# First MLP layer as seven products of half blocks, and the two MLP layers as two stages with their activations in DRAM

## The chip, the cores and the metric

The kernel runs on one core of a Trainium2 chip. Its engines are TensorE (PE in the profile, with its weight loads listed as PEld), VectorE (DVE), ScalarE (ACT), GpSimd (POOL) and SyncE (SP), which issues all DMAs of this kernel. The metric is the time of one execution on the device in microseconds (us), the median of several; lower is better.

## What is computed

An attention over 8 batches, 8 heads, 576 positions of width 64, masked by blocks of 64 positions, is followed by a layer norm and an MLP of two layers (512 to 2048 to 512) with a residual. All inputs and outputs are float32.

```python
scores = scale * np.matmul(q, k.transpose(0, 1, 3, 2))
scores = np.where(block_i >= block_j, scores, -1000000000.0)
attn = np.exp(scores - np.max(scores, axis=-1, keepdims=True))
attn = attn / (np.sum(attn, axis=-1, keepdims=True) + 1e-09)
x = np.matmul(attn, v)            # heads side by side: (8, 576, 512)
xn = (x - mu) / np.sqrt(var + 1e-06) * g_ln
ch = np.maximum(xn @ w_ch1, 0.0) @ w_ch2
return (x + ch).astype(np.float32)
```

The weights arrive as 64-bit words, because the arrays are double precision on the host, and the kernel turns them into float32 on the chip.

## The kernel before

**Order.** Nothing is issued where it is written. Every operation is handed to a planner (`Plan.add`) with its engine or a choice of engines, a cost in us, what it reads and writes, and a priority; `Plan.run` plays the program through with those costs and writes each engine's instructions in the order in which it took them. On the chip each engine then works through its own list strictly in that order and stands still at an instruction whose inputs are not there. A choice of engines (`any_of`, as for the copies out of PSUM in `evac`) is settled by the planner too.

**Attention.** `pair` is called for 32 pairs of heads. On PE a pair is scores (L390), transposes of the softened scores (L417) and the products with the values (L423, L427), with scores one pair ahead of the rest (`pe` and `plan.chain` fix PE's order). DVE takes maxima out of PSUM (L405), ACT the exponentials (L408), both share the copies (L218, L220), and DVE turns the output block (L499, a transpose into `ot`), which SP stores to `xd` in DRAM (L501). `first` does the 64 leading positions of eight pairs at a time. `decode` turns weights into float32 during attention: ACT, POOL, DVE steps on a 128x512 tile (L321 to L333), then a high part (a copy to fp32r, L218 or L220) and a low part (the difference, on POOL, L346), kept in SBUF as `w1h`, `w1l`, `w2h`, `w2l`.

**MLP.** `mlp(n)` handles 4 tiles of 128 tokens, 9 times. Each tile is loaded from `xd`, scaled by the attention's sums (L617), its mean and variance taken (L623, L624), reduced by the mean and multiplied by `g` (L628), turned (L633), stored to and loaded from DRAM in the turned layout, and split into `xh` and `xl`. Then, for each of 16 column blocks j of the hidden layer, PE does 12 matmuls of the first layer (three per 128 rows of input: high by high, high by low, low by high, L680 to L682), ACT and DVE split the rectified result into `hh` and `hl` (L688, L690), and PE does 12 matmuls of the second layer on them (L697 to L699), which add up in PSUM over j. DVE multiplies by the inverse deviation and adds the residual (L706), SP stores (L709). The hidden activations never leave the core.

A matmul of the first layer, and one of the second, move 512 columns:

```python
nc.tensor.matmul(hp.t, w1h[:, c, jf], xh.t[:, c], start=(c == 0), stop=False)
nc.tensor.matmul(ys[s].t, hh.t[:, sl], w2h, start=(j == 0), stop=False)
```

There are 9 x 16 x 12 = 1728 of each layer.

## Time and profile before

| | |
|---|---|
| median of 3 runs | 1100.79 us (1100.09 to 1101.01) |
| profiled execution, first to last instruction (its span) | 1099.8 us |
| PE busy | 1087.7 us, 99% of the span |
| PE weight loads busy | 874.2 us, 79% |
| DVE busy | 517.9 us, 47% |
| ACT busy | 357.5 us, 33% |
| POOL busy | 129.5 us, 12% |

The span is that of one execution, from its first to its last instruction; the times in the first line are of other executions and hold about 1 us more. Busy times are sums of recorded durations. A matmul's recorded duration runs on into that of the next one (they are pipelined), so what a matmul costs in a dense stretch is read from the distance between two starts, not from its duration. The clock column of a window is TensorE's granted clock as a share of 2.4 GHz; 0.50 is its other level, 1.2 GHz.

### The profile page before, as it was taken

What the parts mean: (1) busy time and instruction counts of PE and PEld (TensorE: products, weight loads), DVE (VectorE), ACT (ScalarE), POOL (GpSimd) and SP (SyncE); (2) the same over time, 40 slices, a digit from 0 to 9 for tenths busy, and PEclk for the clock granted to TensorE, in tenths of its full rate; (3) what the DMA queues carried; (4) which work ended last, traced back from release to release, by engine and by line L of the source; (5) the groups of instructions that cost most, each with busy time, mean ns of one, the idle gap of its engine ahead of it and who ended that gap; (6) DMA issues with size and microseconds to landing.
All of it is one profiled execution on the core that took longest, in us unless ns stands there. A gap on an engine that the chain in (4) does not pass through costs nothing.

```text
span 1099.8 us, 16300 instructions
## 1 busy us (share of the span) xinstructions
PE 1087.7 (99%) x6288; PEld 874.2 (79%) x6288; DVE 517.9 (47%) x1192; ACT 357.5 (33%) x884; POOL 129.5 (12%) x192
## 2 busy tenths in 40 slices
PE   9999999999999999999999999999999999999998
PEld 6777777777778888888888888888888888888886
DVE  6899888786775235136126116216315414512111
ACT  8878898898633111111111111111111111111110
POOL 1243432231025101001001001000000100100000
PEclk9999999999999999999999999999999999999999
DMA  6787755655353033024015005104204203301000
GB/s 209 222 217 223 238 190 185 226 168 169 102 129 97 20 78 76 1 63 91 1 43 100 12 1 124 29 1 106 48 1 96 58 1 84 70 1 39 1 1 38
DMA packets 205085, 97.80 MB, mean 89 GB/s; under 512 B 155728, under 2 KB 184400, under 8 KB 205008
## 3 DMA queue, kind: packets, MB, share of 16 engines
q1 hardware_dynamic: 205008, 96.76, 32.3%
q8 instruction: 49, 0.80, 0.3%
q14 instruction: 28, 0.23, 0.1%
...
## 4 chain that ended last, share of the span: by engine, by line
PE 88%; ACT 4%; DVE 4%; DMA 1%; issue 1%; POOL 1%; SPq 0%; DVEq 0%; ACTq 0%; POOLq 0%
PE hp L680 12%; PE hp L682 12%; PE hp L681 12%; PE y L699 12%; PE y L698 11%; PE y L697 11%; PE s L390 5%; PE tr L417 5%; PE o L427 5%; PE o L423 2%; ACT pt L218 1%; ACT pab L408 1%; ACT pu L408 1%; DVE pab L405 1%; DMA st_w2l<-w 1%
## 5 line engine op out<-in xcount | busy, mean ns | idle before, releaser
L690 DVE SCALAR_TENSOR_TENSOR hhl<-hp,hhl 128x512 fp32r<-128x512 f32 x144 | 99.5, 691 | 451.1 <-ACT hhl L688 450.8
L688 ACT ACTIVATE hhl<-hp 128x512 fp32r<-128x512 f32 x144 | 86.1, 598 | 678.3 <-PE hp L682 678.3
L699 PE MATMUL y<-w2h,hhl 128*128 128x512 f32 x576 | 224.4, 390 | 0.3 <-DVE hhl L690 0.3
L698 PE MATMUL y<-w2l,hhl 128*128 128x512 f32 x576 | 224.4, 390 | 0.0
L697 PE MATMUL y<-w2h,hhl 128*128 128x512 f32 x576 | 224.3, 389 | 0.0
L699 PEld LDWEIGHTS y<-w2h,hhl 128*128 128x128 f32 x576 | 108.2, 188 | 23.0 <-DVE hhl L690 0.7
L697 PEld LDWEIGHTS y<-w2h,hhl 128*128 128x128 f32 x576 | 108.1, 188 | 22.4
L698 PEld LDWEIGHTS y<-w2l,hhl 128*128 128x128 f32 x576 | 108.2, 188 | 22.3
L680 PE MATMUL hp<-xq,w1h 128*128 128x512 f32 x320 | 125.1, 391 | 0.0
L682 PE MATMUL hp<-xq,w1l 128*128 128x512 f32 x320 | 124.7, 390 | 0.0
L681 PE MATMUL hp<-xq,w1h 128*128 128x512 f32 x320 | 124.7, 390 | 0.0
L680 PE MATMUL hp<-xp,w1h 128*128 128x512 f32 x256 | 99.7, 390 | 0.0
L682 PE MATMUL hp<-xp,w1l 128*128 128x512 f32 x256 | 99.7, 389 | 0.0
L681 PE MATMUL hp<-xp,w1h 128*128 128x512 f32 x256 | 99.7, 389 | 0.0
L390 PE MATMUL s<-raw 64*128 64x320 f32 (+4 forms) x640 | 94.3, 435 | 0.7 <-DVE nm L405 0.6
L408 ACT ACTIVATE pab<-pab,nm 128x576 f32<-128x576 f32 (+1 forms) x128 | 91.5, 732 | 2.2 <-DVE nm L405 2.2
L390 PEld LDWEIGHTS s<-raw 64*128 64x128 f32 x640 | 57.6, 187 | 38.3 <-issue 32.3
L405 DVE CUSTOM_DVE_ANT_0 pab<-s,never 128x576 f32<-128x576 f32 (+1 forms) x128 | 82.6, 683 | 2.4 <-PE s L390 2.4
L427 PE MATMUL o<-pt,v 128*64 128x256 f32 (+1 forms) x768 | 80.3, 344 | 0.0
L427 PEld LDWEIGHTS o<-pt,v 128*64 128x64 f32 x768 | 56.4, 137 | 26.5
L408 ACT ACTIVATE pu<-pu,nm 128x320 f32<-128x320 f32 (+1 forms) x128 | 64.4, 506 | 30.6 <-DVE nm L405 30.6
L218 ACT COPY pt<-tr 128x512 f32<-128x512 f32 x142 | 73.6, 591 | 2.0 <-PE tr L417 1.4
...
## 6 DMA issues: line engine op xcount, KB each, us to landing
...
xw<-xnt SPq DMA_DIRECT2D x144, 64.0 KB, 1.9
xt<-xw SPq DMA_DIRECT2D x36, 256.0 KB, 2.8
xd<-ot SPq DMA_DIRECT2D x32, 256.0 KB, 3.4
...
```

The lines of the kernel that those rows point to most:

```text
L390: nc.tensor.matmul(x, raw.t[HALF[h], 0, col], raw.t[HALF[h], 1, at:at + x.shape[1]], start=True, stop=True)
L405: add("DVE", dve(n) + .01, lambda: nc.vector.tensor_tensor_reduce(out=p.t[:, part(i, h)], in0=s.t[:, cols], in1=hide, scale=-0.125, scalar ...
L408: add("ACT", act(n, True) + .14, lambda: nc.scalar.activation(out=p.t[:, part(i, h)], in_=p.t[:, part(i, h)], func=AF.Exp, bias=nm.t[:, at ...
L427: nc.tensor.matmul(o.t[HALF[h], at + lo:at + 256], v_sb.t[:, ck, HALF[h]], rhs(h), start=False, stop=(n == len(steps) - 1), skip_group_che ...
L680: nc.tensor.matmul(hp.t, w1h[:, c, jf], xh.t[:, c], start=(c == 0), stop=False)
L681: nc.tensor.matmul(hp.t, w1h[:, c, jf], xl.t[:, c], start=False, stop=False)
L682: nc.tensor.matmul(hp.t, w1l[:, c, jf], xh.t[:, c], start=False, stop=(c == NC - 1))
L688: add("ACT", act(TW), lambda hp=hp, hh=hh: nc.scalar.activation(out=hh.t, in_=hp.t, func=AF.Relu), r=[hpart], w=[hh], alloc=[hhl], prio=0)
L690: add("DVE", dve(TW), lambda hp=hp, hh=hh, hl=hl: nc.vector.scalar_tensor_tensor(out=hl.t, in0=hp.t, scalar=0.0, in1=hh.t, op0=ALU.max, op ...
L697: nc.tensor.matmul(ys[s].t, hh.t[:, sl], w2h, start=(j == 0), stop=False)
L698: nc.tensor.matmul(ys[s].t, hh.t[:, sl], w2l, start=False, stop=False)
L699: nc.tensor.matmul(ys[s].t, hl.t[:, sl], w2h, start=False, stop=(j == NJ - 1))
```

## The change

**Stages.** The program has three stages now: attention, the first layer for all tokens, the second layer for all tokens. SBUF room is passed on by a `Phase`: the tiles of attention lie in a pool `attn`, those of the first layer's operands (`op`, `quad`, `s1x`, `s2x`) in a pool `inner`, which opens where `attn` has closed, on the same addresses.

**First layer.** `prep` takes 6 tiles of tokens (768, two halves of 384), 6 times. The preparation of a tile is as before, but the normalised value is complete here (mean and inverse deviation in one instruction, L689), `g` is folded into the weights (in `decode1`, on POOL), and the residual is stored to DRAM (`xres`). From the quarter blocks (384 tokens by 256 inputs) of a superblock it forms four sums or differences of 128x768 (L711, L712, L714, L728) and splits seven operands into high and low (`operand`, L356 for the low part). `decode1` forms the seven weight operands. `quad` does the seven products for the column blocks q and q + 8: each is 6 matmuls of 384 columns (L755) into three PSUM blocks a, b, c. ACT copies two results (L764, L769), DVE forms five sums of 128x384 (L762) of a PSUM block and a part of the SBUF tile `quad`, and SP stores the four finished blocks to `hd` in DRAM. PE's order is chained: the first two products of a quad, the last two of the quad before, then three more.

**Second layer.** `outer` takes 384 tokens, 12 times: it loads `hd`, splits the rectified values on ACT and DVE (L833, L835), and does 9 matmuls of 512 columns per column block (L842 to L844). The second layer's weights are decoded during the first layer (`decode2`), kept in DRAM, and split into SBUF where the first layer's weights lay.

**Counts on PE.** Attention's instructions on PE are the same, in the same order. The first layer has 6 x 8 x 7 x 6 = 2016 matmuls of 384 columns, the second 12 x 16 x 9 = 1728 of 512.

```diff
-BT = 4
+HT = 384
-YO = 13
-D_0, D_1 = 12.0, 1.1
+D_0, D_1 = 1.0, 3.0
...
+class Phase:
+
...
+    def __init__(self, enter, before=None):
+        self.enter, self.before, self.left, self.guard, self.pool = enter, before, 0, None, None
+
+    def ready(self):
+        return self.pool or self.before is None or not self.before.left
+
+    def open(self):
+        if self.pool is None:
+            if self.before:
+                self.before.close()
+            self.guard = self.enter()
+            self.pool = self.guard.__enter__()
+        return self.pool
+
+    def close(self):
+        self.guard.__exit__(None, None, None)
...
+                            x.tile is None and (x.phase and not x.phase.ready() or x.after and x.after.tile is None
+                                                and x.after not in k.allocs)
+                    for p in k.phases:
+                        p.left -= 1
...
+    new_tr, new_s1, new_o, new_acc = (kind(n, [P, 512], F32, 4, psum, "tr") for n in ("tr", "s1", "o", "acc"))
...
+    new_w1 = [kind("w1", [P, 2, 7, 2 * P], F32R, 1, None, f"w{q}") for q in range(8)]
+    new_w2 = [kind("w2", [P, 3, 2, DM], F32R, 1, None, f"w{q}") for q in range(6)]
+    new_pt0 = [kind("pt0", [P, 2, 4, 2, P], F32, 1, None, f"w{q}") for q in (6, 7)]
+    new_word, new_hhl = kind("word", [P, 2048], I32, 2), kind("hhl", [P, 2, 2, HT], F32R, 2, None, "word")
+    new_xab, new_hin = kind("xab", [P, NC, HT], F32, 2), kind("hin", [P, 4, HT], F32, 2, None, "xab")
+    new_quad2, new_res1 = kind("quad2", [P, 4, HT], F32, 1), kind("res1", [P, 3, DM], F32, 1, None, "quad2")
+    new_x, new_w2f, new_res0 = (kind(n, [P, DM], F32, 3, None, "x") for n in ("x", "w2f", "res0"))
+    new_xn, new_xnt = kind("xn", [P, DM], F32, 1), kind("xnt", [P, DM], F32, 1)
...
+    new_pab = kind("pab", [P, 2048], F32, 2, attn)
...
+    new_op = kind("op", [P, 2, 2, HT], F32R, 7, inner)
+    new_quad = kind("quad", [P, 4, HT], F32, 2, inner)
+    new_s1x, new_s2x = kind("s1x", [P, 2, HT], F32, 1, inner), kind("s2x", [P, 2, HT], F32, 1, inner)
...
+    xres = [kind("xres", [P, DM], F32, NT, dram)() for _ in range(NT)]
+    hd = [kind("hd", [2 * NJ * P, HT], F32, NSB, dram)() for _ in range(NSB)]
+    w2d = [kind("w2d", [P, DM], F32, NJ, dram)() for _ in range(NJ)]
...
+    def split(hi, lo, src, n, r, out, prio, pool_only=False):
...
+        h, l = Buf(parent=out), Buf(parent=out)
+        add(any_of(lambda e: copy(e, hi(), src()), ACT=act(n, True), DVE=.12 + n / 1920),
+            r=r, w=[h], prio=prio)
+        add(any_of(lambda e: e.tensor_sub(lo(), src(), hi()), **({} if pool_only else {"DVE": dve(n)}), POOL=pool(n)),
+            r=[*r, h], w=[l], prio=prio)
+        return [h, l]
...
+    def decode1(q, prio):
...
+            add("POOL", pool(512), lambda w=w: nc.gpsimd.tensor_mul(
+                w().rearrange("p (c n) -> p c n", c=NC), w().rearrange("p (c n) -> p c n", c=NC),
+                g_sb.unsqueeze(2).to_broadcast([P, NC, P])), r=[full, gb], w=[scaled], prio=prio)
...
+        for n, (x, y, r) in enumerate(((b12, b11, [b0, b1]), (b22, lambda: t(0), [b1, ts[0]]), (b22, b12, [b1]),
+                                       (b21, lambda: t(1), [b0, ts[1]]))):
+            add("POOL", pool(256), lambda n=n, x=x, y=y: nc.gpsimd.tensor_sub(t(n), x(), y()),
+                r=r, w=[ts[n], word], prio=prio)
...
+    def decode2(j, prio):
+        stage, word, full, w = decode(lambda out: nc.sync.dma_start(out=out, in_=w2[j]), prio)
+        there = Buf(parent=w2d[j])
+        load(P * 2048, lambda: nc.sync.dma_start(out=w2d[j].t, in_=w()), r=[full], w=[there], prio=prio)
+        return there
+
+    for q in range(6):
+        decode1(q, 100 + 10 * (D_0 + D_1 * q))
...
+    for q in (6, 7):
+        decode1(q, 100 + 10 * NPAIR + q)
+    base = 100 + 10 * NPAIR
...
+    def prep(sb_):
...
+                load(P * 2048, lambda x=x, t=t: nc.sync.dma_start(out=xres[t].t, in_=x.t), r=part, w=[kept], prio=prio)
...
+                add("DVE", .15 + 512 / 1920, lambda x=x, s=s, xn=xn, norm=norm: nc.vector.tensor_scalar(
+                    out=xn.t, in0=x.t, scalar1=norm.t[:, 2 * s:2 * s + 1], scalar2=norm.t[:, 6 + s:7 + s],
+                    op0=ALU.subtract, op1=ALU.mult), r=[*part, mv, rstd], w=[xn], prio=prio)
+                add("DVE", dve(512), lambda xn=xn, xnt=xnt: nc.vector.transpose(xnt.t, xn.t), r=[xn], w=[xnt], prio=prio)
...
+        s1, s2 = new_s1x(), new_s2x()
+
+        def both(fn, **kw):
+            add(any_of(fn, DVE=dve(n), POOL=pool(n)), **kw)
+        both(lambda e: e.tensor_add(flat(s1.t), lo2(B_), hi2(B_)), r=[a21, a22], w=[s1], prio=p1)
+        both(lambda e: e.tensor_sub(flat(s2.t), flat(s1.t), lo2(A)), r=[s1, a11], w=[s2], prio=p1)
+        s3 = Buf(parent=B_)
+        both(lambda e: e.tensor_sub(lo2(B_), lo2(A), lo2(B_)), r=[a11, a21], w=[s3, a21], prio=p1)
+        ops = {}
+
+        def operand(name, src, r):
+            o = new_op()
+            part = lambda h: lambda: flat(o.t[:, h])
+            ops[name] = o, split(part(0), part(1), src, n, [r], o, p1)
+        operand(1, lambda: lo2(A), a11)
+        operand(6, lambda: flat(s2.t), s2)
+        operand(5, lambda: flat(s1.t), s1)
+        operand(2, lambda: hi2(A), a12)
+        operand(7, lambda: lo2(B_), s3)
+        operand(4, lambda: hi2(B_), a22)
+        s4 = Buf(parent=s1)
+        both(lambda e: e.tensor_sub(flat(s1.t), hi2(A), flat(s2.t)), r=[a12, s2], w=[s4, s1], prio=p1)
+        operand(3, lambda: flat(s1.t), s4)
+        return ops
...
+    def quad(g, ops):
+        sb_, q = divmod(g, 8)
+        wq, parts = w1_of[q]
+        if g % 2 == 0:
+            a, b, c = new_acc(), new_acc(), new_acc()
+            at = [lambda x=x: x.t[:, 0:HT] for x in (a, b, c)]
+        else:
+            two = new_y2(), new_y2()
+            a, b, c = Buf(parent=two[0]), Buf(parent=two[0]), Buf(parent=two[1])
+            at = [lambda k=k: two[k // 2].t[:, k % 2 * 512:k % 2 * 512 + HT] for k in range(3)]
+        pa, pb, pc = at
+        out = (new_quad2 if g % 3 == 2 else new_quad)()
+
+        def product(n, acc, where, start):
+            o, ready = ops[n]
+
+            def go():
+                for k in range(2):
+                    w = lambda h: wq.t[:, h, (0, 1, 2, 6, 3, 4, 5)[n - 1], P * k:P * k + P]
+                    x = lambda h: o.t[:, h, k]
+                    for i, (wi, xi) in enumerate(((0, 0), (0, 1), (1, 0))):
+                        nc.tensor.matmul(where(), w(wi), x(xi), start=start and k == 0 and i == 0,
+                                         stop=k == 1 and i == 2, skip_group_check=True)
+            return add("PE", 6 * (HT / 2400 + MMO), go, r=[*ready, *parts[n - 1]], w=[acc], prio=1e6 + g)
...
+        def sum_(o, where, x, r, w):
+            add("DVE", dve(HT) + .09, lambda: nc.vector.tensor_add(slot(o)(), where(), slot(x)()), r=r, w=w, prio=0)
+        t1 = product(1, a, pa, True)
+        add("ACT", act(HT), lambda: nc.scalar.copy(out=slot(2)(), in_=pa()), r=[a], w=[p1], prio=0)
+        t6 = product(6, b, pb, True)
+        sum_(1, pb, 2, [b, p1], [u2])
+        t5 = product(5, c, pc, True)
+        t2 = product(2, a, pa, False)
+        add("ACT", act(HT), lambda: nc.scalar.copy(out=slot(0)(), in_=pa()), r=[a], w=[c11], prio=0)
+        t7 = product(7, b, pb, False)
+        sum_(3, pb, 2, [b, p1], [u3])
+        sum_(3, pc, 3, [c, u3], [c22])
+        t4 = product(4, b, pb, False)
+        sum_(2, pb, 2, [b, p1], [c21])
+        t3 = product(3, c, pc, False)
+        sum_(1, pc, 1, [c, u2], [c12])
+        there = Buf(parent=hd[sb_])
+        load(P * 4 * HT * 4, lambda: nc.sync.dma_start(
+            out=hd[sb_].t.rearrange("(x q p) n -> q p x n", q=8, p=P)[q], in_=out.t), r=[c11, c12, c21, c22], w=[there],
+            prio=1)
+        hparts.setdefault(sb_, []).append(there)
+        return [t1, t6], [t5, t2, t7], [t4, t3]
...
+    for sb_ in range(NSB):
+        ops = prep(sb_)
+        for q in range(8):
+            first2, mid, end = quad(8 * sb_ + q, ops)
+            order += [*first2, *late, *mid]
+            late = end
+        for j in range(len(w2_there), min(NJ, len(w2_there) + 4)):
+            w2_there.append(decode2(j, base + 8 * sb_ + 6 + .3 * (j % 4)))
+    plan.chain(order + late)
...
+    for j in range(NJ):
+        if j % 3 == 0:
+            w = new_w2[j // 3]()
+        f, at = new_w2f(), j % 3
+        load(P * 2048, lambda j=j, f=f: nc.sync.dma_start(out=f.t, in_=w2d[j].t), r=[w2_there[j]], w=[f], prio=prio)
+        w2_of.append((part(0), part(1), split(part(0), part(1), lambda f=f: f.t, DM, [f], w, prio)))
...
+    def outer(n):
...
+            x = Buf(parent=three, view=lambda t, s=s: t[:, s]) if half else new_res0()
+            load(P * 2048, lambda t=t, x=x: nc.sync.dma_start(out=x.t, in_=xres[t].t), r=[kept_of[t]], w=[x], prio=prio + .8)
...
-                def hmm(c=c, hp=hp, q=q, jf=jf):
-                    w1h, w1l = weights["w1h", q].tile, weights["w1l", q].tile
-                    nc.tensor.matmul(hp.t, w1h[:, c, jf], xh.t[:, c], start=(c == 0), stop=False)
-                    nc.tensor.matmul(hp.t, w1h[:, c, jf], xl.t[:, c], start=False, stop=False)
-                    nc.tensor.matmul(hp.t, w1l[:, c, jf], xh.t[:, c], start=False, stop=(c == NC - 1))
...
+            if j % 4 == 0:
+                h = new_hin()
+                load(P * 4 * HT * 4, lambda h=h, j=j: nc.sync.dma_start(
+                    out=h.t, in_=hd[sb_].t.rearrange("(j p) n -> p j n", p=P)[:, NJ * half + j:NJ * half + j + 4]),
+                    r=hparts[sb_], w=[h], prio=prio + .05 * j)
+            if j % 2 == 0:
+                two_j = new_hhl()
...
+            add("ACT", act(HT, True), lambda o=o, src=src: nc.scalar.activation(out=o.t[:, 0], in_=src(), func=AF.Relu),
+                r=[h], w=[hh], prio=prio + .05 * j)
+            add("DVE", dve(HT), lambda o=o, src=src: nc.vector.scalar_tensor_tensor(
+                out=o.t[:, 1], in0=src(), scalar=0.0, in1=o.t[:, 0], op0=ALU.max, op1=ALU.subtract),
+                r=[h, hh], w=[hl], prio=prio + .05 * j)
...
+                    hi, lo = w2_of[j][0](), w2_of[j][1]()
+                    nc.tensor.matmul(ys[s].t, o.t[:, 0, sl], hi, start=(j == 0), stop=False)
+                    nc.tensor.matmul(ys[s].t, o.t[:, 0, sl], lo, start=False, stop=False)
+                    nc.tensor.matmul(ys[s].t, o.t[:, 1, sl], hi, start=False, stop=(j == NJ - 1))
+                add("PE", 3 * (512 / 2400 + MMO), ymm, r=[hh, hl, *w2_of[j][2]], w=[ys[s]], prio=at + 10 * j + .1 * s)
...
+            add("DVE", dve(512), lambda s=s, x=x: nc.vector.tensor_add(x.t, ys[s].t, x.t), r=[ys[s], x], w=[done], prio=2)
```

**Order on PE at the end of attention.** Before, transposes and value products of the last pair, with first-layer matmuls between them:

```order
L417 MATMUL tr<-ident,pab 128x128 x12
L680 MATMUL hp<-xq,w1h_340 128x512
L681 MATMUL hp<-xq,w1h_340 128x512
L682 MATMUL hp<-xq,w1l_343 128x512
L417 MATMUL tr<-ident,pab 128x128 x4
L423 MATMUL o<-pt_3748,v 64x256 x2
```

After, the same stretch and the start of the first layer (`acc` and `y` are the PSUM blocks of even and odd quads, `w_244` and `w_464` the weight operands of q = 0 and 1):

```order
L459 MATMUL tr<-ident,pab 128x128 x16
L465 MATMUL o<-pt_4023,v 64x256 x2
L469 MATMUL o<-pt_4023,v 64x256 x2
L469 MATMUL o<-pt_4023,v 64x128 x2
L465 MATMUL o<-pt_4040,v 64x256 x2
L469 MATMUL o<-pt_4040,v 64x256 x6
L469 MATMUL o<-pt_4040,v 64x128 x2
L755 MATMUL acc<-op,w_244 128x384 x30
L755 MATMUL y<-op,w_464 128x384 x12
L755 MATMUL acc<-op,w_244 128x384 x12
```

No MLP matmul stands between attention's any more, and the first product stands behind the last value product.

**Order on DVE there.** Before, from the last block's transpose on:

```order
L499 STREAM_TRANSPOSE ot<-o 128x512
L633 STREAM_TRANSPOSE xnt<-xn 128x512
L690 SCALAR_TENSOR_TENSOR hhl<-hp,hhl 128x512
L617 TENSOR_TENSOR xre<-xre,sums_all 128x512 x2
L623 BN_STATS st<-xre 128x6
```

After, from the same transpose on:

```order
L541 STREAM_TRANSPOSE ot<-o 128x512
L711 TENSOR_TENSOR s1x<-xab 128x768
L712 TENSOR_TENSOR s2x<-s1x,xab 128x768
L714 TENSOR_TENSOR xab<-xab 128x768
L356 TENSOR_TENSOR op<-xab,op 128x768
L356 TENSOR_TENSOR op<-s2x,op 128x768
L356 TENSOR_TENSOR op<-s1x,op 128x768
L356 TENSOR_TENSOR op<-xab,op 128x768 x2
L762 TENSOR_TENSOR quad<-acc,quad 128x384
L356 TENSOR_TENSOR op<-xab,op 128x768
L728 TENSOR_TENSOR s1x<-xab,s2x 128x768
L343 SCALAR_TENSOR_TENSOR word<-word 128x512
```

Three sums of 128x768 stand ahead of the first product's low part now, and the six other low parts follow with the first sums and a decoding step between them. `s1x` and `op` lie on addresses of `attn`, so the first instruction on them waits for all of attention's reads and stores there, the store of `ot` to `xd` among them.

**Order on DVE inside the first layer.** Before, a stretch of `mlp` (`xq` a split input, `xre` a residual):

```order
L690 SCALAR_TENSOR_TENSOR hhl<-hp,hhl 128x512
L220 CAST xq<-xt 128x4x128
L648 TENSOR_TENSOR xq<-xt,xq 128x4x128
L690 SCALAR_TENSOR_TENSOR hhl<-hp,hhl 128x512 x9
L706 SCALAR_TENSOR_TENSOR xre<-y,norm,xre 128x512 x4
```

After, at the change from one superblock to the next:

```order
L762 TENSOR_TENSOR quad<-y,quad 128x384 x2
L356 TENSOR_TENSOR op<-xab,op 128x768
L728 TENSOR_TENSOR s1x<-xab,s2x 128x768
L343 SCALAR_TENSOR_TENSOR word<-word 128x512
L692 STREAM_TRANSPOSE xnt<-xn 128x512
L762 TENSOR_TENSOR quad_4744<-acc,quad_4744 128x384
L356 TENSOR_TENSOR op<-s1x,op 128x768
L762 TENSOR_TENSOR quad_4744<-acc,quad_4744 128x384
```

The sums that read PSUM (L762) stand in one list with the making of operands, the decoding of weights (L343) and the preparation of tiles (L692).

## Rows read from the trace of the kernel before

**Rows 1.** Part 1 of the page: busy time, share, instructions of each engine.

```profile
PE 1087.7 (99%) x6288; PEld 874.2 (79%) x6288; DVE 517.9 (47%) x1192; ACT 357.5 (33%) x884; POOL 129.5 (12%) x192
```

**Rows 2.** Windows: length, busy PE, PEld, DVE, ACT, POOL, clock, DMA share, GB/s.

```profile
5.00:313.00 308.00, 302.07 (x2827) 223.64 (x2826) 254.83 (x742) 260.62 (x716) 81.03 (x68) 1.00 0.62 191
313.00:1095.20 782.20, 781.91 (x3449) 647.23 (x3447) 260.52 (x446) 95.64 (x167) 47.83 (x118) 1.00 0.21 47
1095.20:1099.70 4.50, 0.02 (x1) 0.00 (x0) 1.50 (x3) 0.00 (x0) 0.00 (x0) 0.73 0.60 233
```

**Rows 3.** Timeline at attention's end and the program's: start, length, engine, line, operation.

```profile
302.65 0.50 PE L680 MATMUL hp<-xq,w1h 128*128 128x512 f32 x1
...
311.37 1.68 PE L427 MATMUL o<-pt,v 128*64 128x256 f32 x16
...
312.98 0.51 PE L680 MATMUL hp<-xq,w1h 128*128 128x512 f32 x1
...
313.10 0.72 DVE L499 STREAM_TRANSPOSE ot<-o 128x512 f32<-128x512 f32 x1 [0.90 <-PE o L427]
...
1094.83 0.39 PE L699 MATMUL y<-w2h,hhl 128*128 128x512 f32 x1
```

**Rows 4.** Groups by line and form on PE: count, busy us, mean ns, idle before.

```profile
L699 PE MATMUL y<-w2h,hhl 128*128 128x512 f32 x576 | 224.4, 390 | 0.3 <-DVE hhl L690 0.3
...
L680 PE MATMUL hp<-xq,w1h 128*128 128x512 f32 x320 | 125.1, 391 | 0.0
...
L680 PE MATMUL hp<-xp,w1h 128*128 128x512 f32 x256 | 99.7, 390 | 0.0
```

**Rows 5.** Transposes on the timeline, and two groups of weight loads.

```profile
215.10 1.91 PE L417 MATMUL tr<-ident,pab 128*128 128x128 f32 x16
...
L417 PEld LDWEIGHTS tr<-ident,pab 128*128 128x128 f32 x512 | 56.5, 141 | 5.3 <-ACT pt L218 2.9 <-DVE pt L220 0.8 <-issue 0.3
...
L680 PEld LDWEIGHTS hp<-xq,w1h 128*128 128x128 f32 x320 | 60.1, 188 | 12.6 <-issue 0.3
```

**Rows 6.** DMA issues: KB of one, median us from issue to landing.

```profile
xd<-ot SPq DMA_DIRECT2D x32, 256.0 KB, 3.4
...
out_t<-xrf SPq DMA_DIRECT2D x20, 256.0 KB, 2.0
```

**Rows 7.** Groups by line and form on DVE.

```profile
L405 DVE CUSTOM_DVE_ANT_0 pab<-s,never 128x576 f32<-128x576 f32 x64 | 48.0, 751 | 2.4 <-PE s L390 2.4
...
L405 DVE CUSTOM_DVE_ANT_0 pu<-s,never 128x192 f32<-128x192 f32 x64 | 22.5, 351 | 0.0
...
L617 DVE TENSOR_TENSOR xre<-xre,sums_all 128x512 f32<-128x512 f32 x16 | 11.1, 700 | 2.1 <-DMA xre<-xd 2.1
...
L690 DVE SCALAR_TENSOR_TENSOR hhl<-hp,hhl 128x512 fp32r<-128x512 f32 x144 | 99.5, 691 | 451.1 <-ACT hhl L688 450.8
...
L330 DVE SCALAR_TENSOR_TENSOR st_w2h<-st_w2h 128x512 int32<-128x512 int32 x14 | 10.7, 766 | 4.0 <-ACT st_w2h L326 4.0
...
L333 DVE SCALAR_TENSOR_TENSOR st_w2h<-st_w2h 128x512 int32<-128x512 int32 x14 | 9.8, 703 | 0.3 <-POOL st_w2h L324 0.3
...
L623 DVE BATCH_NORM_STATS2 st<-xre 128x6 f32<-128x512 f32 x16 | 11.0, 690 | 0.3
...
L624 DVE BATCH_NORM_AGGREGATE norm<-st 128x2 f32<-128x6 f32 x36 | 6.6, 182 | 1.2
...
L633 DVE STREAM_TRANSPOSE xnt<-xn 128x512 f32<-128x512 f32 x36 | 25.2, 701 | 3.9 <-DMA xw<-xnt 3.8
...
L220 DVE CAST xq<-xt 128x512 fp32r<-128x512 f32 x20 | 8.5, 423 | 13.2 <-DMA xt<-xw 13.2
```

**Rows 8.** Windows after PE's last matmul, and the warm-up transposes by form.

```profile
1096.00:1098.00 2.00, 0.00 (x0) 0.00 (x0) 0.70 (x2) 0.00 (x0) 0.00 (x0) 0.82 1.02 396
1098.00:1099.80 1.80, 0.00 (x0) 0.00 (x0) 0.00 (x0) 0.00 (x0) 0.00 (x0) 0.50 0.14 55
...
L280 PE MATMUL tr<-ident 128*128 128x128 f32 x16 | 3.7, 421 | 1.3 <-POOL ident masks.py:199 1.3
```

374 lines of the change are left out of this document (168 added, 206 removed).

## The prediction

> **What bounds the kernel now.** I read the page's first part, then the windows by stage. PE is busy 99% of the span, the others at most 47% [rows 1]. The windows say where that share comes from [rows 2]: from 5 to 313 us is attention, with PE busy 302.1 of 308.0, but DVE 254.8 and ACT 260.6 close behind; from 313 to 1095.2 is the MLP, with PE busy 781.9 of 782.2, DVE 260.5 and ACT 95.6; then 4.5 us of last additions and stores. So PE sets the pace in both stages. In the MLP DVE idles two thirds of the time, in attention a sixth. The timeline gives the borders [rows 3]: attention's last value products start at 311.37 and last 1.68, to 313.05; a dense stretch of 512-column matmuls begins at 312.98, and its last one starts at 1094.83. There are 3456 such matmuls (three lines of 576 in each layer [rows 4]); 9 of them, in threes like the one at 302.65 [rows 3], lie inside attention, in holes of PE. So 3447 take 1094.83 + 0.23 - 312.98 = 782.1 us, 0.2269 each.
>
> **PE's work in the two layers.** The second layer keeps 1728 matmuls of 512 columns: 1728 x 0.2269 = 392.1. The first now has 2016 of 384 columns, a form the trace does not hold. From below: if all of a matmul's cost goes with its columns, 0.75 x 0.2269 = 0.1702. From above: 16 transposes of 128 columns take 1.91 us, of which the last one's recorded 0.27 runs out behind it, so they start 0.109 apart [rows 5]; the line through (128, 0.109) and (512, 0.2269) gives 0.1876 at 384. I take 0.1736, a fifth of the way up from the low end, since the 512-column matmul is the same operation on the same types and the transpose is not. That makes 2016 x 0.1736 = 350.0 and 742.1 for both layers, against 782.1: **40.0 us less** (2016 x 0.0034 = 7 better at the low end, 28 worse at the high one). The weight load must fit beneath: one is recorded with 188 ns, longer than 173.6, but the transposes' loads are recorded with 141 and follow each other every 109 [rows 5], so a recorded length overlaps the next by 32 at least, and 188 - 32 = 156 fits.
>
> The Trainium skill, page "TensorE: Matmul & The Clock Gate", section "Back-to-back issue gap", puts the gap of an isolated warm matmul at N/2.4 + 2.5 ns, 216 for 512 columns, where this trace has 226.9. By that rule, as an estimate, 384 columns would take 162.5 ns and the sum would be 22 us lower; the trace has already left the rule at 512, so I don't follow it.
>
> **The door between attention and the first layer.** Before, MLP matmuls stood ready behind attention; the dense stretch begins with no gap at 312.98 [rows 3]. Now the first operands lie on attention's addresses. The chain is: last value product ends at 313.05; DVE turns the block, 0.05 + 0.72 [rows 3]; SP issues the store (I allow 0.2), which has to land, 3.4 in the median [rows 6], so 317.4. Only then may DVE begin with three sums and the first low part, four operations of 768 columns. Their price: 576 and 192 columns took 751 and 351 ns [rows 7], 1.04 ns a column and 0.15 fixed, so 0.95 for 768; with two operands in SBUF 512 took 700 [rows 7] where the line gives 684, so 0.97. Four are 3.9: product 1 has only its first matmul until 321.3. PE loses 8.3. Then DVE delivers a low part every 0.97, about what a product takes (6 x 0.1736 = 1.04), but the products 4 and 3 of quad 0 wait for sums, the fourth difference and the decoding step that stand ahead of the last low parts in DVE's list: 2 us more. And the clock: after the last matmul of the program the granted clock is 0.82 on average from 1096 to 1098 and 0.50 after that [rows 8], so a gap of 8 us ends at half speed; the 16 warm-up transposes at 421 ns against 0.109 apart later [rows 5, 8] show what a slow start looks like, 3.7 us for what else takes 1.9. I take 1 of these 1.8, since PE waits for DVE meanwhile anyway. Together **11 us** (6 if the store lands in 2.0, like those of the output [rows 6], and the late waits hide; 20 if the two weight loads issued just ahead of it delay it and PE stays slow).
>
> The same page, section "Part 1: The HAM clock gate", says that the lower clock is the default which activity lifts; the trace agrees (0.50 once PE stands still). It speaks against putting a gap into a dense stretch.
>
> **DVE and the rest inside the first layer.** By superblock PE has 336 x 0.1736 = 58.3 us. DVE's list, counted from the order: 40 sums of 384 columns at 0.15 + 384 x 0.00104 = 0.55 (the line above; its source is PSUM too, and 512 from PSUM and SBUF took 691 [rows 7], where it gives 684), 22.0; about 11 operations of 768 at 0.97, 10.7 (17 in the first superblock, which makes its own operands late and the next one's early); decoding steps at 0.735 (the mean of 766 and 703 [rows 7]), 14, 14, 8 and then none; and by tile scaling 0.70, statistics 0.87, normalising 0.42 if it goes like the copy of 423 (0.75 if like a three-operand one), turning 0.70 [rows 7]. Sums: 57, 56, 51, 49, 34 and 41 us. So for two superblocks DVE is as full as PE, for two more nearly, and it is a list in fixed order: a sum that PE waits for stands behind whatever began before it. PE has slack for that: between the end of product 7 and the start of 4, which needs the sum in between, lie two products, 2.1 us, against a longest DVE step of 0.97. At the change of superblocks, where seven low parts come within some 16 us, the slack goes. I charge **6 us**, a little over 1 per superblock (0 to 35; the top end is the rival below). ACT has two copies a quad and half of the splits, less than half of DVE's sum, and POOL a few decoding steps. DMA: the store of a quad is 786 KB in 7.2 us, 109 GB/s, with the tiles' traffic besides; attention moves 191 at 0.62 of the engines [rows 2]. It fits, and a quad's buffer comes round only every third quad.
>
> **Attention.** Its PE list is unchanged, so its end moves only if others fall behind. From the order DVE has 24 decoding steps fewer, but 14 more tiles' statistics, 12 more normalisings, 10 more scalings, 11 more transposes and 11 more copies: at the prices above some 18 us more, 273 of 308; ACT has those decoding steps and copies fewer. Still below PE: **+2 us** (-1 to +10).
>
> **Second layer and end.** 9 matmuls a column block, 2.04 us, against one DVE step of 0.55 and one ACT step. The first of its weights are split while the last quads run, in the room of those that are done with. The end is as before: last additions and a store.
>
> **Sum**, against the profiled execution: 1099.8 - 782.1 + 742.1 + 11 + 6 + 2 = 1078.8; the median of the runs lies 1.0 above its span, so **1079.8 us**, 20 us or 1.8% less. A half of what PE saves goes at the door and on DVE.
>
> **The rivals.**
> *Columns don't set the cost (slower).* If a 384-column matmul can't start before its weight load's recorded end, 0.188 apart, the first layer takes 2016 x 0.188 = 379.0, 29 more: 1108.8. It decides from 0.184 (1100.8) on. For it: 188 is longer than the stream [rows 5], and the line through the transposes gives the same 0.188. Against it: the overlapping loads of the transposes. 10%.
> *DVE sets the pace.* If waits in its list make the first four superblocks' 213 us into 260, they end at 317.4 + 260 = 577.4, where PE alone would be at 313.05 + 233.2 = 546.3: 31 lost instead of 17, 1094. At 267, a quarter more, the gain is gone; at 277 it is 1111. For it: the counts above. Against it: sums go first when ready, and POOL is free. 16%, of which 9 below, 3 within and 4 above the kernel before.
> *The fixed part falls away with shorter streams.* If the stream takes one clock a column at the granted 2.4 GHz (1.00 in [rows 2]), 0.2133 of the 0.2269 is stream and 0.0136 a fixed part; should the shorter form be free of it, 384 columns take 0.160 and PE 2016 x 0.0136 = 27 us less, of which DVE in the full superblocks gives 10 back: 1063. Against it: the 512-column form pays that part in the densest stretch of the trace. 6%. The rule of the page "TensorE: Matmul & The Clock Gate" of the Trainium skill named above, with 2.5 ns of fixed part, points to this case.
> *Attention falls behind* by 10 us, for DVE at 89% and the tiles' loads in SP's list: 1090. 6%.
>
> **How the numbers follow.** The forecast has 62%, between 1068 and 1095 by its own bounds. Leaving out the slower rival (10) and the upper part of DVE's (7), the range is 1061 to 1101. A measurement of this kernel can tell 0.2%, 2.2 us, from no change. Faster: 62 + 6 + 6 + 9 = 83%; within: 3%; slower: 10 + 4 = 14%.
>
> **What would show it.** Starts of the 384-column matmuls 0.17 apart in a dense stretch (0.19: the first rival). A hole of some 8 us on PE at 313, ended by DVE's low part behind the landing of `ot`, and a granted clock below 1 there. PE's idle time inside the first layer put down to DVE at the first four superblocks, with DVE busy over 85% there, and almost none in the last two. The second layer dense at 0.227. Wrong would be: DVE never idle and PE waiting in every quad, or the second layer waiting for weights.

## The result, and the profile after

The changed kernel takes 1091.1 us in the median of its six runs (1090.1 to 1097.8), the kernel before 1100.9: 0.992 of it, with a 95% interval of 0.990 to 0.994. So it is faster by under 1%, clear of the noise, but by 9.7 us where the prediction had 21.0; the time lies inside the range. The profiled execution spans 1089.6 us against 1099.8.

Part 1 of the page, and then the windows by stage, with the columns of [rows 1, 2]: attention, the door, the rest of the first layer, the second layer, the end. (The door is what the prediction calls the passage from attention to the first layer; a superblock is the 768 tokens that one `prep` prepares.)

```profile
PE 1056.9 (97%) x6576; PEld 901.8 (83%) x6576; DVE 664.5 (61%) x1497; ACT 436.3 (40%) x1054; POOL 174.8 (16%) x266
```

```profile
5.00:325.30 320.30, 306.54 (x2817) 222.58 (x2816) 273.65 (x790) 244.04 (x682) 111.50 (x157) 1.00 0.76 201
325.30:340.00 14.70, 6.29 (x21) 5.88 (x20) 9.85 (x12) 7.35 (x11) 3.26 (x2) 0.65 0.21 66
340.00:693.20 353.20, 349.83 (x2005) 347.04 (x2005) 260.22 (x469) 95.25 (x172) 59.34 (x101) 1.00 0.79 226
693.20:1083.60 390.40, 390.40 (x1724) 323.04 (x1722) 118.31 (x223) 88.42 (x188) 0.00 (x0) 1.00 0.43 138
1083.60:1089.60 6.00, 0.15 (x1) 0.00 (x0) 1.40 (x3) 0.00 (x0) 0.00 (x0) 0.82 0.36 134
```

The timeline of the changed kernel (start, length, engine, line, operation, in brackets the idle time before and what ended it): attention's last value product, the door, a dense stretch of the first layer, the last matmul.

```profile
324.71 0.60 PE L469 MATMUL o<-pt,v 128*64 128x256 f32 x6
325.36 0.72 DVE L541 STREAM_TRANSPOSE ot<-o 128x512 f32<-128x512 f32 x1 [2.56 <-PE o L469]
326.11 0.34 SPq L543 DMA_DIRECT2D xd<-ot  x1
330.25 0.96 DVE L711 TENSOR_TENSOR s1x<-xab 128x768 f32<-128x768 f32 x1 [4.18 <-DMA xd<-ot]
330.29 0.83 ACT L244 CAST op<-xab 128x768 fp32r<-128x768 f32 x1 [7.48 <-DMA xd<-ot]
331.17 0.69 PE L755 MATMUL acc<-op,w 128*128 128x384 f32 x1 [5.86 <-ACT op L244]
...
333.41 0.95 DVE L356 TENSOR_TENSOR op<-xab,op 128x768 fp32r<-128x768 f32 x1
334.41 7.84 PE L755 MATMUL acc<-op,w 128*128 128x384 f32 x29 [2.55 <-DVE op L356]
342.09 2.24 PE L755 MATMUL y<-op,w 128*128 128x384 f32 x12
344.17 1.03 PE L755 MATMUL acc<-op,w 128*128 128x384 f32 x5
...
1083.37 0.39 PE L844 MATMUL y<-w,hhl 128*128 128x512 f32 x1
```

Read against [rows 3]: attention ends at 324.71 + 0.60 = 325.3, where it ended at 313.05: 12.3 us late. The door is as foretold: turn, store, landing, the first copy at 330.29, one matmul at 331.17 and the next only at 334.41, behind the low part of 333.41. In the dense stretch 12 matmuls of 384 columns start between 342.09 and 344.17, 0.173 apart.

For the account I use the starts of the 3744 dense matmuls. A matmul's own step is 0.1733 (384 columns) or 0.2269 (512), so 2016 x 0.1733 + 1728 x 0.2269 = 741.5 us, 40.6 less than the 782.1 before. *Door*: from attention's end to the first product's first matmul, plus what the steps of the next 10 us exceed 0.1733. *Stalls*: the excess in the rest of the first layer. The changed kernel has 5.9 + 5.7 = 11.6 at the door and 5.6 of stalls. Attention +12.3, door +11.6, stalls +5.6, the end +1.3 (6.3 us from the last matmul's start, before 5.0 [rows 3]), matmuls -40.6, second layer -0.3: -10.1, against -10.2 in the spans. Nearly the whole miss is attention.

VectorE in the first two superblocks of the first layer (window, length, VectorE busy, clock, DMA share, GB/s):

```profile
331.20:398.20 67.00, 53.06 (x89) 0.93 0.77 207
398.20:458.80 60.60, 50.04 (x93) 1.00 1.00 283
```

VectorE's waits in attention (engine, tile and line, what it waited for: us in total, times, longest), the largest of the kernel before and then those of the changed kernel that matter:

```profile
DVE ot L499 <- PE o L427: 31.2, 20, 2.9
```

```profile
DVE ot L541 <- PE o L469: 14.9, 13, 2.6
DVE x L656 <- DMA x<-xd: 7.1, 5, 2.5
...
DVE xnt L692 <- DMA x<-xd: 2.8, 3, 1.7
...
DVE xnt L692 <- DMA xw<-xnt: 1.8, 1, 1.8
...
DVE st L665 <- DMA x<-xd: 1.3, 1, 1.3
DVE x L656 <- DMA xw<-xnt: 1.2, 1, 1.2
```

The idle time behind the value products, which is spare time, has shrunk from 31.2 to 14.9 us. In its place are 14.2 us before instructions of the tile preparation whose transfer has not landed (2.1 before, [rows 7]). While VectorE stands there, the score reductions and copies out of PSUM behind it in its list wait too, and then TensorE. Three rows of attention show that chain: ScalarE's wait for VectorE's maxima, before and after, and TensorE's largest wait after, for copies that ScalarE makes.

```profile
ACT pu L408 <- DVE nm L405: 30.6, 18, 4.7
```

```profile
ACT pu L450 <- DVE nm L447: 51.7, 21, 6.1
...
PE tr L459 <- ACT pt L244: 4.1, 8, 1.0
```

TensorE's waits in attention sum to 5.6 us before and to 12.7 after. Compared one by one, its 2832 matmuls up to attention's end lose 10.7 of the 12.3 us in front of the transposes of the softened scores (L459), the instruction of that last row. The planner that writes the lists reckons a 64 KB transfer on an idle line as landed 0.6 + 0.65 + 0.22 + 1.5 = 3.0 us after its issue began (issue, LAG, size by BW, TAIL); the trace has, in attention (KB each, median us to landing):

```profile
x<-xd SPq DMA_DIRECT2D x76, 64.0 KB, 4.8
```

**Theory A**: these waits are attention's delay. **B**: it is the first weights, now decoded from the first pair on. **C**: it is the tiles' work or their traffic as such.

### The profile page after: what moved, and what is told of

Read it like the earlier page. It is cut to its first block, busy times and chain, and to the rows that moved or that the text cites. A ratio compares the mean times of both kernels' runs of the same rounds, so it can differ in the third digit from the quotient of the medians.

```text
span 1089.6 us, 17956 instructions
## 1 busy us (share of the span) xinstructions
PE 1056.9 (97%) x6576; PEld 901.8 (83%) x6576; DVE 664.5 (61%) x1497; ACT 436.3 (40%) x1054; POOL 174.8 (16%) x266
## 4 chain that ended last, share of the span: by engine, by line
PE 66%; DMA 3%; DVE 2%; SPq 1%; POOL 1%; issue 1%; ACT 1%; DVEq 0%; ACTq 0%; POOLq 0%
PE acc L755 14%; PE y L755 13%; PE acc L844 6%; PE acc L843 6%; PE acc L842 6%; PE y L844 6%; PE y L843 6%; PE y L842 6%; DMA x<-xd 1%; PE tr L459 1%; PE o L469 1%; PE s L432 1%; DMA xw<-xnt 1%; SPq L696 1%; DMA xab<-xw 1%
## 5 line engine op out<-in xcount | busy, mean ns | idle before, releaser
L835 DVE SCALAR_TENSOR_TENSOR hhl<-hin,hhl 128x384 fp32r<-128x384 f32 x192 | 98.6, 554 | 250.2 <-ACT hhl L833 250.2
L833 ACT ACTIVATE hhl<-hin 128x384 fp32r<-128x384 f32 x192 | 90.3, 517 | 298.4 <-PE acc L844 153.4
L755 PE MATMUL acc<-op,w 128*128 128x384 f32 x1008 | 190.6, 338 | 11.6 <-ACT op L244 5.9
L755 PEld LDWEIGHTS acc<-op,w 128*128 128x128 f32 x1008 | 178.1, 190 | 14.1 <-ACT op L244 6.1
L755 PE MATMUL y<-op,w 128*128 128x384 f32 x1008 | 186.8, 334 | 0.2 <-DVE quad L762 0.2
L755 PEld LDWEIGHTS y<-op,w 128*128 128x128 f32 x1008 | 175.6, 188 | 0.9 <-DVE quad L762 0.9
L844 PE MATMUL acc<-w,hhl 128*128 128x512 f32 x288 | 112.1, 389 | 0.0
L843 PE MATMUL acc<-w,hhl 128*128 128x512 f32 x288 | 112.1, 389 | 0.0
L842 PE MATMUL y<-w,hhl 128*128 128x512 f32 x288 | 112.0, 389 | 0.0
L844 PE MATMUL y<-w,hhl 128*128 128x512 f32 x288 | 112.0, 389 | 0.0
L843 PE MATMUL y<-w,hhl 128*128 128x512 f32 x288 | 112.0, 389 | 0.0
L842 PE MATMUL acc<-w,hhl 128*128 128x512 f32 x288 | 112.0, 389 | 0.0
L762 DVE TENSOR_TENSOR quad<-y,quad 128x384 f32<-128x384 f32 x120 | 65.7, 552 | 47.1 <-ACT quad L769 22.9
L762 DVE TENSOR_TENSOR quad<-acc,quad 128x384 f32<-128x384 f32 x120 | 65.7, 551 | 23.1 <-PE acc L755 22.5
L459 PE MATMUL tr<-ident,pab 128*128 128x128 f32 x512 | 68.0, 277 | 9.3 <-ACT pt L244 4.1
```

The source lines that it names most:

```text
L459: nc.tensor.transpose(o.t[:, n * P:(n + 1) * P], x, ident)
L755: nc.tensor.matmul(where(), w(wi), x(xi), start=start and k == 0 and i == 0, stop=k == 1 and i == 2, skip_group_check=True)
L762: add("DVE", dve(HT) + .09, lambda: nc.vector.tensor_add(slot(o)(), where(), slot(x)()), r=r, w=w, prio=0)
L833: add("ACT", act(HT, True), lambda o=o, src=src: nc.scalar.activation(out=o.t[:, 0], in_=src(), func=AF.Relu), r=[h], w=[hh], prio=prio + ...
L835: add("DVE", dve(HT), lambda o=o, src=src: nc.vector.scalar_tensor_tensor(out=o.t[:, 1], in0=src(), scalar=0.0, in1=o.t[:, 0], op0=ALU.max ...
L842: nc.tensor.matmul(ys[s].t, o.t[:, 0, sl], hi, start=(j == 0), stop=False)
```

## The experiments

All are edits of the changed kernel; an added line shifts the line numbers. Times in us; end, door and stalls as worked out above (a + marks a single run).

| kernel | attention ends | door | stalls | last matmul | time | ratio to before, 95% |
|---|---|---|---|---|---|---|
| before | 313.1 | | | 1094.8 | 1100.9 | |
| changed | 325.3 | 11.6 | 5.6 | 1083.4 | 1091.1 | 0.992 (0.990 to 0.994) |
| e1 tiles later | 313.4 | 10.5 | 81.3 | 1146.0 | 1154.4 | 1.049 (1.047 to 1.051) |
| e2 told longer | 317.7 | 12.9 | 10.9 | 1082.3 | 1086.5 | 0.987 (0.985 to 0.988) |
| e6 told shorter | 340.5 | 10.9 | 19.1 | 1111.4 | 1118.0+ | |
| e3 decode at 12 | 325.8 | 10.4 | 8.5 | 1085.7 | 1092.0 | 0.992 (0.990 to 0.993) |
| e5 moves alone | 336.0 | 10.3 | 81.4 | 1168.6 | 1175.3+ | |
| e9 moves paced | 315.4 | 11.8 | 82.1 | 1150.3 | 1156.9+ | |
| e10 work alone | 318.2 | 10.5 | 81.1 | 1150.7 | 1158.1+ | |
| e4 last ot apart | 323.8 | 7.2 | 5.6 | 1077.4 | 1084.8 | 0.986 (0.984 to 0.987) |
| e7 hole filled | 321.5 | 12.3 | 9.2 | 1083.9 | 1092.8 | 0.993 (0.991 to 0.995) |
| e8 combined | 316.7 | 3.9 | 7.1 | 1068.6 | 1075.0 | 0.976 (0.975 to 0.978) |
| e11 and weights | 316.4 | 4.1 | 7.1 | 1068.5 | 1075.7 | 0.976 (0.975 to 0.978) |
| e12 two ahead | 316.3 | 4.3 | 25.6 | 1087.1 | 1094.4 | 0.994 (0.992 to 0.996) |

Attention's end scatters: the changed kernel, e3, e4 and e7 do nearly the same there in somewhat different lists, and end between 321.5 and 325.8. A difference of 2 us in one pair of lists says little. Nor does the end follow VectorE's waits for transfers among these four: they are 14.2 us in the changed kernel, 10.7 in e3, 14.8 in e4 and 12.2 in e7.

### Attention: e1, tiles later

```
+        hold = xparts[B - 1][:4] if sb_ else []
...
-                            r=xparts[b], w=[part[u]], alloc=[x], prio=prio)
+                            r=xparts[b] + hold, w=[part[u]], alloc=[x], prio=prio)
```

(and the same for the tiles out of `xd0`)

> The tiles of superblocks 1 to 5 are loaded only when attention's last block has been stored; only superblock 0's six tiles are prepared during attention (19 tiles' statistics before that in the changed kernel). Theory A (VectorE's list stands in front of instructions whose tile transfers have not landed; 14.2 us of such idle time in the changed kernel's attention) and theory C (the sheer work and traffic of 13 more tiles): attention's last value product ends at 314 to 317 instead of 325.3. Theory B (the first weights are decoded from the first pair on, where they used to come from the twelfth): it stays at 323 to 326. The 13 tiles move into the first layer, some 2.7 us of VectorE each, so stalls there should go from 5.3 us to between 10 and 35, and the time come out between 1082 and 1105.

Attention ends at 313.4, where it ended before the change: the delay is the early tiles, not the weights. But the stalls are 81 us, more than twice what I allowed. TensorE's waits in e1's first layer:

```profile
PE acc L756 <- ACT op L244: 48.0, 5, 23.9
```

Five waits, one at each change of superblock: the next superblock's first operand is late. They are 48 of the 81 us; part of the rest is the clock behind such holes, with 0.92 granted between 330 and 760. In the stretch of the longest wait, VectorE is busy 17.2 us of 31 (window, columns as in [rows 2]):

```profile
383.00:414.00 31.00, 3.11 (x11) 2.02 (x9) 17.22 (x31) 6.82 (x12) 10.26 (x9) 0.57 0.99 263
```

So it is not the sum of VectorE's work that fails to fit into a superblock. What is late is the chain of the tiles (load, scale, statistics, root, normalise, turn, store, load, sum, split) with its transfers. Whether it is late by the number of its steps or because the DMA engines are full (a share of 0.99 here, while a tile's load of 64 KB landed 2.6 us after its issue in the median) no run tells apart. The early tiles are needed.

### Attention: e2 and e6, the planner told longer and shorter

```
-        add("SP", .6, fn, size=nbytes, **kw)
+        k = add("SP", .6, fn, size=nbytes, **kw)
+        k.wait = LONGER if kw["prio"] in TILES else 0.0
...
-                        late = line + TAIL - busy[eng]
+                        late = line + TAIL + k.wait - busy[eng]
```

`TILES` holds the priorities of the tile preparation; `LONGER` is 2.5 in e2 and -1.5 in e6.

> The planner is told that the tiles' transfers land 2.5 us later, so that their users come later in the lists; the work and the traffic stay. Theory A: VectorE's idle time before instructions that wait for transfers falls from 14.2 us in attention to under 4, attention ends at 314 to 319, and the time is 1079 to 1085. Theories B and C: attention ends at 323 to 326 as before, the time is 1088 to 1091.

> The opposite of e2: the planner is told that the tiles' transfers land 1.5 us sooner than it thought. Theory A: VectorE's idle time on transfers in attention grows from 14.2 us to over 18, and attention ends at 327 to 334. Against it: if e2's gain came from another order by chance, attention stays within 323 to 327.

VectorE's waits in attention, e2 (the row of the spare time; no row names a DMA) and e6:

```profile
DVE ot L546 <- PE o L474: 22.4, 16, 2.6
```

```profile
DVE ot L546 <- PE o L474: 12.9, 10, 2.6
DVE x L661 <- DMA x<-xd: 10.4, 6, 2.3
...
DVE st L670 <- DMA x<-xd: 7.9, 2, 4.2
DVE xnt L697 <- DMA xw<-xnt: 5.8, 3, 3.0
```

Waits for transfers of 0, 14.2 and 24.1 us go with ends at 317.7, 325.3 and 340.5. In e2 nearly the same work and traffic stand in the same stretch (in VectorE's list before the last block, 18 tiles' statistics instead of 19, 11 scalings instead of 13, 2 weight copies more). So theory A holds, for some 7.6 of the 12.3 us, give or take the scatter above. Of the 4.6 that are left, up to 1.8 (an estimate, 60 x 0.03) can be the clock: in e2 0.97 was granted from 120 to 180, in the changed kernel 1.00. The median falls by 4.6 and not by 7.6, and misses its range: stalls rise by 5.3 in the profiled execution and the door by 1.3, with one step of 3.3 us before the last superblock's first operand as the largest. e6 moves attention the other way, by 15.2 us, further than I expected.

### Attention: e3, the weights' times of before

```
-D_0, D_1 = 1.0, 3.0
+D_0, D_1 = 12.0, 1.1
```

> The first weights are decoded from the twelfth pair on, 1.1 pairs apart, as in the kernel before, everything else as in the changed kernel. Theory B: attention ends at 314 to 318 instead of 325.3 and the time is 1079 to 1084. Theories A and C: attention ends at 322 to 327, since the tiles come into the same stretch, and the time is 1087 to 1092.

Attention ends at 325.8, the time is the changed kernel's: theory B falls.

### What is left: e5, e9 and e10, traffic alone and work alone

All three start from e1. e5 and e9 add, per tile, the same moves between DRAM buffers that nothing reads (shortened):

```
+        for u in range(4):
+            load(P * 512, <xd to dum0, 128-byte pieces>, r=xparts[b], w=[got[u]], prio=prio)
+        load(P * 2048, <dum0 to dum1>, r=got, ...)
+        for g4 in range(4):
+            load(32 * 2048, <dum0 to dum2, 128-byte pieces>, r=got, ...)
```

In e9 the first of them also wait for the pair `PACE[t]` (`r=xparts[b] + pace`). e10 instead has the tiles' instructions on VectorE and GpSimd, fed from the constant `never`.

> As e1 (attention's end at 313.4), but the transfers that went with the 13 tiles come back to attention as moves between DRAM buffers that nothing reads: 52 of 64 KB in pieces of 128 bytes, 13 of 256 KB, 40 of 64 KB in pieces of 128 bytes, in tile order in SyncE's list; no engine works on them. It tells which part of what e2 left over (attention still 4.6 us later than before) is traffic and which is work. Traffic on the DMA engines and in SyncE's list (theory C, first form): attention ends at 316 to 320. VectorE's and GpSimd's work on the tiles (theory C, second form): 313 to 315. The first layer is as slow as in e1, and the time some 1150, by both.

> As e5, but each tile's unread moves now wait for the pair behind which the tile's loads stand in the changed kernel (tile 6 behind pair 12, tile 18 behind pair 27), so that amount, pieces and spacing are those of the changed kernel, and no engine waits for them. e5's 22.6 us would be the price of a burst: then attention ends at 314 to 317 here. If traffic at this amount costs by itself what e2 left over (4.6 us) or more: 317 to 326. The first layer is as in e1 by both, the time 1150 to 1165.

> As e1, but VectorE and GpSimd do the work of the 13 tiles in attention (13 scalings, 13 statistics, 10 normalisings, 10 turnings, 4 root steps) on data that are already in SBUF, at the same places and without any transfer; nothing reads the result. Work on the engines as the cause: attention ends at 316 to 325. Waits for transfers and traffic as the cause: 313 to 315.5. The time is 1150 to 1165 by both.

e5 missed its interval by 16 us: 22.6 us for moves that no engine waits for. With the same moves spaced out (e9) it is 2.0. So the amount alone isn't what costs; unpaced, the moves come in clumps, and transfers that are needed land late. TensorE's waits in e5's attention show the scores' operands among them, and ScalarE's the weight words:

```profile
PE s L432 <- DMA raw<-qk: 7.0, 3, 6.2
...
ACT word L336 <- DMA word<-w: 13.3, 4, 7.6
```

The longest wait for scores' operands can be followed. SyncE issues without a pause from 202 on, mostly moves, at 0.5 to 1 us each. The load stands among them. It is issued at 209.41 and lands 5.6 us later, about as in the changed kernel (5.4 in the median). So it was late because it was issued late, in SyncE's list:

```profile
202.11 4.12 SPq L639 DMA_DIRECT2D dum<-xd  x4
...
209.41 0.56 SPq L421 DMA_DIRECT2D raw<-qk  x1
...
215.16 4.66 PE L432 MATMUL s<-raw 64*128 64x320 f32 x20 [6.23 <-DMA raw<-qk]
```

Part of e5's delay is the clock: over attention 0.97 was granted, in e9 0.99 (an estimate of at most 331 x 0.03 = 10 us). e10 costs 4.8 us, and that is not work alone: VectorE also waits 4.2 us there for superblock 0's own tiles, where e1 has 0.8. e9's traffic costs 2.0 (within the scatter). Together that is 6.8, near the 4.3 that e2 has over e1. Roughly, then, the 12 us are up to 5 of work, 0 to 2 of traffic, and the rest waits in a fixed list; with one run and one list for each price, this split is an estimate.

### The door: e4, the last block apart

```
+    new_ot_end = kind("ot", [P, 512], F32, 1, None, "quad2")
...
-        ot = new_ot()
+        ot = new_ot_end() if k == NPAIR - 1 else new_ot()
```

> Only the last pair's output block gets memory outside attention's pool, so the first layer's operands wait for the last value product and no longer for the store of that block to land. Theory D (the landing, 4.1 us after the block is turned, sets the door): the first matmul of the first layer starts 1.5 to 2.5 us behind the last value product instead of 5.9, the door costs 7 to 9 us instead of 11.6, and the time is 1085 to 1088. Rival E (making sums and operands sets it anyway): the door stays at 11 to 12, the time at 1088 to 1091. Attention's end stays at 325 under both.

The timeline of e4: last value product, the first sum and copy, the first and second matmul of product 1.

```profile
322.72 1.04 PE L470 MATMUL o<-pt,v 128*64 128x256 f32 x10
...
323.86 0.96 DVE L712 TENSOR_TENSOR s1x<-xab 128x768 f32<-128x768 f32 x1 [2.62 <-PE o L470]
323.92 0.83 ACT L244 CAST op<-xab 128x768 fp32r<-128x768 f32 x1 [2.67 <-PE o L470]
324.81 0.44 PE L756 MATMUL acc<-op,w 128*128 128x384 f32 x1 [1.05 <-ACT op L244]
...
328.20 2.29 PE L756 MATMUL acc<-op,w 128*128 128x384 f32 x6 [2.95 <-DVE op L357]
```

The first matmul comes 1.05 us behind attention instead of 5.86: the landing of the store was 4.8 us of the hole (theory D), and the door falls by 4.4, to 7.2. What remains are the sums, the turned block and the first low part on VectorE, until 328.20. The time falls by 6.3 us, to just under the range expected; 1.5 of that is an earlier end of attention, which I don't ascribe to the edit.

### The door: e7, the hole filled

```
+        for _ in range(HOLE):
+            nc.tensor.transpose(awake.t[:, 0:P], ident, ident)
...
+    plan.chain([max(steps.items())[1][-1], fill, order[0]])
```

> 75 transposes of 128 columns that nothing reads stand on TensorE between attention's last value product and the first product, 8.2 us of work in a hole of 9. If the 0.31 us steps of the first product's matmuls come from the clock, they become 0.17 and the granted clock stays at 1.0: the time falls by 2 to 3 us, to 1088 to 1089.5. If they are waits for operands, they stay and the time is 1091 to 1092.

Windows behind the hole, first the changed kernel, then e7 (columns as in [rows 2]), and e7's timeline:

```profile
330.00:335.00 5.00, 1.28 (x3) 0.88 (x4) 4.71 (x5) 4.71 (x7) 1.78 (x1) 0.50 0.02 3
335.00:340.00 5.00, 5.00 (x18) 5.00 (x17) 4.42 (x7) 2.64 (x5) 1.48 (x1) 0.51 0.00 0
340.00:345.00 5.00, 5.00 (x30) 5.00 (x30) 3.04 (x6) 1.84 (x4) 1.04 (x1) 1.00 0.77 221
```

```profile
330.00:335.00 5.00, 4.53 (x24) 3.92 (x23) 5.00 (x6) 3.62 (x6) 1.63 (x1) 1.00 0.00 0
335.00:340.00 5.00, 2.19 (x12) 2.19 (x13) 5.00 (x9) 1.21 (x2) 0.69 (x1) 1.00 0.65 182
```

```profile
321.47 8.41 PE L799 MATMUL acc<-ident 128*128 128x128 f32 x75
...
330.51 4.47 PE L756 MATMUL acc<-op,w 128*128 128x384 f32 x23 [0.46 <-DVE op L357]
337.81 1.33 PE L756 MATMUL acc<-op,w 128*128 128x384 f32 x6 [2.83 <-DVE quad L763]
```

The clock reading is confirmed, the gain is not. The granted clock stays at 1.00 and the steps of 0.32 us are gone; but TensorE then reaches the first sum that VectorE owes it and waits 2.8 us, with VectorE busy 5.00 of 5. In the changed kernel the 2.6 us of slow steps had covered this wait. The door costs 12.3 us against 11.6, and the time is no better than the changed kernel's (1092.8 against 1091.1), although attention happened to end 3.8 us earlier; 3.6 us more of stalls behind the door stand against that.

### Together: e8, e11 and e12

e8 has e2's edit for the first four superblocks' tiles only, and one buffer `edge` in `quad2`'s place for the last block and superblock 0's first sum:

```
+        ot = new_ot() if k < NPAIR - 1 else Buf(parent=edge, view=lambda t: t[:, 768:1280])
...
+        s1 = new_s1x() if sb_ else Buf(parent=edge, view=lambda t: t[:, 0:768].rearrange("p (k n) -> p k n", k=2))
```

> Three edits together: the planner is told 2.5 us more for the transfers of the first four superblocks' tiles (those that fall into attention), the last pair's output block lies apart from attention's pool, and the first of superblock 0's sums does too, so that it is made early. Theory A and D: attention ends at 317 to 319, the first matmul of the first layer follows within 1.5 us, the door costs 2 to 5 us in all instead of 11.6, the stalls behind it 4 to 8; the time is 1072 to 1078. If the parts get in each other's way: 1079 to 1086.

The timeline of e8's door:

```profile
315.70 1.04 PE L477 MATMUL o<-pt,v 128*64 128x256 f32 x10
...
316.90 0.83 ACT L246 CAST op<-xab 128x768 fp32r<-128x768 f32 x1 [2.46 <-PE o L477]
...
317.79 0.44 PE L764 MATMUL acc<-op,w 128*128 128x384 f32 x1 [1.05 <-ACT op L246]
...
318.78 1.66 PE L764 MATMUL acc<-op,w 128*128 128x384 f32 x6 [0.55 <-DVE op L362]
```

Door 3.9, no wait of VectorE for a transfer in attention, 1075.0 us: 2.4% under the kernel before and 16 us under the changed one. Both the waits and the door were mended with the change's own work left as it is.

e11 told the planner the weights' loads too: `load(...).wait = LONGER if prio < TILES[0] else 0.0`.

> e8, and the planner is told 2.5 us more for the loads of the first weights in attention too, whose users on ScalarE waited up to 3 us in e2. If those waits are what is left of attention's delay (316.7 against 313.05): attention ends at 313.5 to 315.5 and the time is 1071 to 1074. If it is work or traffic: 316 to 318 and 1073.5 to 1076.5.

ScalarE's waits for weight words fall from 10.0 us in e8 to 1.7, but attention's end and the time stay (316.4, 1075.7): the 3.4 us of attention that are left are not those waits. e10's 4.8 us suggest work, and e8's granted clock of 0.97 from 120 to 180 a share of TensorE's lower level; neither is shown.

e12 is e8 with e1's hold for superblocks 2 and later (`if sb_ > 1`).

> e8, but only the twelve tiles of superblocks 0 and 1 are prepared during attention; the tiles from 12 on are loaded once the last block is stored. Six tiles' statistics and four normalisings less lie in attention, where e10 and e9 priced 13 tiles at 4.8 and 2.0 us: attention ends 1 to 3 us earlier, at 314 to 316. If one superblock ahead is enough for the first layer, its stalls stay at 5 to 10 and the time is 1071 to 1075. If the chain of a superblock's tiles takes longer than the superblock before it, as e1's waits of 24 to 3 us at its changes suggest, stalls go to 15 to 45 and the time to 1080 to 1110.

Attention's end hardly moved (316.3), and stalls went to 25.6: one wait of 12.5 us for the third superblock's first operand, the first whose tiles come late:

```profile
PE acc L765 <- ACT op L246: 16.9, 3, 12.5
```

Two superblocks prepared in attention are not enough.

## Why the prediction was wrong, step by step

- **PE's work: right.** 0.173 us a matmul was foretold at 0.1736, 40.6 us saved at 40.0. *Columns don't set the cost* falls: the load's recorded 190 ns overlap the next matmul's, as [rows 5] suggested. *The fixed part falls away* falls too: the line through (384, 0.1733) and (512, 0.2269) is 0.419 ns a column and 12.5 ns fixed, so the shorter form pays the fixed part of the longer. The Trainium skill, page "TensorE: Matmul & The Clock Gate", section "Back-to-back issue gap", gives N/2.4 + 2.5 ns for an isolated matmul, as an estimate 162.5 for 384 columns; the measured 173 decides, as 227 did for 512.
- **Attention: +2 was the step that failed; it is +12.3.** The prediction summed VectorE's work (273 us, and the window above shows 273.65) and, finding it below TensorE's, charged almost nothing. That a list in fixed order also waits was a thought applied to the first layer, and not to attention, where the new instructions have a DMA in front of each and where 31.2 of the list's 53 us of idle time were those behind value products. The rival *Attention falls behind* had the place and the size (10 us, 1090) and 6%; of its two reasons, VectorE's load is worth at most about 5 us (e10), and the tiles' loads cost through the waits for them in VectorE's list (e2, e6), hardly by their place in SyncE's list when they are spread as here (e9).
- **The door: right in its main term and in the sum, 11.6 for 11.** The hole was 9.1 us from attention's end to the second matmul (8.3 foretold): the block's store took from 326.11 to 330.25, 4.1 us where I had 0.2 + 3.4. e4 confirms the landing. The last 3 us were foretold as 2 of waits for late low parts and sums and 1 for the clock; the trace has 2.6 of slow steps and no such wait. e7, at the full clock, has the wait (2.8) in place of the slow steps: either one hides the other, and that the two terms came to the right sum is luck.
- **Stalls in the first layer: right, 5.6 for 6.** VectorE was busy 53, 50, 47, 46, 32 and 40 us by superblock (57, 56, 51, 49, 34 and 41 foretold). In the two fullest it worked 53 of 67.0 us and 50 of 60.6, about 80%, not 98. TensorE's waits behind the door, 3.3 us, are all for VectorE's results and all before 470. *DVE sets the pace* did not happen. What can stall this stage is the chain of the tiles, which the prediction didn't weigh: e1 and e12 have stalls of 81 and 26 us, the lower clock behind the holes included.
- **Second layer and end**: the second layer is dense at 0.227, the end 1.3 us longer than before.

So the sums for the matmuls, the door and the stalls held within 1 us, and the one that failed is worth nearly all of the difference: -21.0 + 10.3 = -10.7, against -9.7.
